# A first dense pair cut into chunks of 512, 512 and 128 tokens, with banks given out by first free

## The chip, the cores and the metric

The kernel runs on one core of a Trainium2 chip. The metric is the device time of one execution in microseconds. In the rows, PE is TensorE (matmuls; PEld its weight loads), DVE is VectorE, ACT is ScalarE, POOL is GpSimd and SP is the engine that issues most plain DMAs.

## What is computed

A small attention over 32 memory slots gives a row of 512 numbers for each of 4608 tokens. A mixture of 8 experts follows: each token goes to one expert, each expert takes 576 tokens, and runs two matrix products with a ReLU between them. Then one dense layer, the same for all tokens, with a product, a gate and a product:

```python
x = attn_out                      # 4608 x 512
for e in range(8):                # 576 tokens each, by sorted router logits
    h = np.maximum(x[mask_e] @ w1[e], 0.0)      # 512 -> 1024
    out[mask_e] = h @ w2[e]                     # 1024 -> 512
h = out @ w_in                    # 512 -> 2048
g = h * np.clip(h + 3.0, 0.0, 6.0) / 6.0
return g @ w_out                  # 2048 -> 512
```

Products run in two 16-bit parts of each operand, so each of them is three matmuls: high by high, high by low, low by high.

## The kernel before

The attention comes first (to about 230 us). Then experts are taken in pairs. For each expert `l1` makes 16 tiles of 288 tokens (12 matmuls each) and `l2` makes 8 (24 matmuls each); after both experts of a pair, `l34(P)` runs the dense layer over the pair's 1152 tokens. `l34` has three chunks of 384 tokens and, in each, 16 steps `f` of the hidden dimension. A step has an L3 part (12 matmuls with the 128x128 tiles of `w_in` as weights and the chunk's tokens moving, into one PSUM bank `p`) and an L4 part (3 matmuls for each 128 tokens, into accumulators `acc0` to `acc2` that live for the whole chunk). Between them the step is evicted: ScalarE makes the gate from `p`, VectorE multiplies it by `p` (which frees the bank), ScalarE casts the high part `g[:, 0]`, GpSimd subtracts to get the low part. `LAG = 2`: the L4 part of step n is issued after the L3 part of step n+2. At a chunk's end the accumulators go through ScalarE and VectorE and are scattered to the output.

Engines take their instructions in the order in which a planner wrote them down. The planner keeps a clock (`CK.now`) and an estimate of each engine's time (`V_`, `A_`, `G_`); generators for routing, gathering, weights and dense weights are run as side tasks while the matmuls are recorded, and a task goes on when the estimate says its turn has come. What is late on the chip against that plan makes the in-order queues wait.

Four side tasks matter here:

- `weights()` loads the 8 x 2 expert matrices into four staging buffers `wst0` to `wst3`, takes a scale (the matmul `amx` spreads the maximum over partitions) and converts them into `w_0` to `w_3`. W1[e] and W2[e] below are the first and second matrix of expert e.
- `route(k)` finds the tokens of the k-th expert: eight rounds of compare and count, then six one-hot tiles `OH` on VectorE, each used by six small matmuls `rtp`, and at the end the row numbers `ix`.
- `gathers()` fetches the token rows `xg` by an indirect DMA on GpSimd and transposes them (`xp`) into `xt`.
- `dense_piece` turns one of 32 pieces of `w_in` and `w_out` from their 64-bit words into two 16-bit parts. A piece has four VectorE instructions on a `cva` buffer (one TENSOR_SCALAR and three SCALAR_TENSOR_TENSOR), three on ScalarE and one subtract on GpSimd. Pieces of `w_out` can't be finished before their scale is known (`dmx`, after all of `w_out` has been looked through by `dm`). L3 of step f needs piece f of `w_in` (`WI[f]`), L4 needs piece f of `w_out`.

`ysplit` scales an expert's output for the dense layer: the maxima `ym` of its 8 tiles go into `sy_1m` for the second expert of a pair, and one matmul `amx` waits for that. This `amx` stands in TensorE's queue behind the first L3 matmuls of the chunk, though the first chunk holds only tokens of the pair's first expert.

PSUM has eight banks: four under the tag `mm` (all of `p`, `amx`, `xp`), `acc0` to `acc2`, and one for `rtp`. `mm` banks are given out in turn: a new tile waits for the oldest of the four.

Of the kernel before, what the change touches and what calls it, by code (L numbers as in the profile page):

```python
# [20 lines left out]
def attn_moe_kernel(ctx: ExitStack, tc: tile.TileContext, q, k, v, phi, w_gate, w1, w2, w_in, w_out, out):  # L21
    nc = tc.nc
# [67 lines left out]
    with tc.tile_pool(name="ald", bufs=2) as ald, tc.tile_pool(name="aw", bufs=2) as aw, \  # L90
# [322 lines left out]
        def x_mm(t, pool, tag, *gs):  # L413
            u, half = XO[t // 2], t % 2
            if gs != (1,):
                XP[t] = pool.tile([128, 2, 256], F32, name="xa", tag=tag, bufs={"qp": 2, "mm": 4}[tag])
# [212 lines left out]
    MMQ = []  # L629

    def mm_slot(done):
        while len(MMQ) >= 4:
            d = MMQ.pop(0)
            b, CK.busy = CK.busy, False
            need(lambda: d[0])
            CK.busy = b
        MMQ.append(done)

    def mm_tile(shape, name, done):
        mm_slot(done)  # L640
        return ps.tile(shape, F32, name=name, tag="mm", bufs=4)
# [23 lines left out]
    ones72 = rt.tile([128, 2 * NT], F32, name="ones72")  # L665
    nc.vector.memset(ones72, 1.0)
# [21 lines left out]
    def all_max(m, f, late=0.0):  # L688
        yield V_.t + HOP + late
        done = [False]  # L690
        while len(MMQ) >= 4 and not MMQ[0][0]:
            yield CK.now + 0.05
# [44 lines left out]
    def route(k):  # L737
# [136 lines left out]
        V_.tensor_tensor_scan(sc.rearrange("p a t -> p (a t)"), ones72, G.rearrange("p a t -> p (a t)"), 0.0,  # L874
# [51 lines left out]
        def oh(q4):  # L926
            o = rt.tile([128, 6, 128], BF16, name="OH", bufs=3)
# [3 lines left out]
        yield V_.t - 0.3  # L931
        OH = [oh(0)]
# [51 lines left out]
    def weights():  # L984
        for T in range(2 * E):
            k, which = divmod(T, 2)
            while k not in EIX or T == 3 and 1 not in XI:
                yield CK.now + 0.3
# [26 lines left out]
            for n in range(9):  # L1015
# [19 lines left out]
                elif n:  # L1035
# [5 lines left out]
                    if i and T + 1 < 2 * E and T != 2:  # L1041
                        w_issue(T + 1, c)
# [5 lines left out]
    XT, XI = {}, set()  # L1048
# [7 lines left out]
    def gathers():  # L1056
        for k in range(E):
# [7 lines left out]
            def fetch(i):  # L1065
# [3 lines left out]
                elif k == 1 and i > 1:  # L1069
                    if i % 2 == 0:  # L1070
                        big.append(wk.tile([128, 2, 512], F32, name="xg", tag=f"wst{i // 2 - 1}"))
                    xg = big[-1][:, i % 2]
                else:
                    xg = wk.tile([128, 512], F32, name="xg", tag=f"xg{i % 2}")
# [3 lines left out]
            depth = 2 if k > 1 else 5  # L1078
            big = []
# [7 lines left out]
            XI.add(k)  # L1087
# [4 lines left out]
            for i in range(5):  # L1092
# [4 lines left out]
                while len(MMQ) >= 4 and not MMQ[0][0]:  # L1097
# [49 lines left out]
    def spare(kind):  # L1147
        tags = ["dst0", "dst1", "dst2"] if kind else ["cva0", "cva1"]
        if 1 in XT or 1 in L1D:
            tags += [] if kind else ["xg0", "xg1"]  # L1150
# [102 lines left out]
    def x_tiles(n):  # L1253
        for _ in range(n):
# [4 lines left out]
            if g == 0:  # L1259
                XC[:] = [[False]]  # L1260
                mm_slot(XC[0])
            x_mm(t, ps, "mm", g)
# [130 lines left out]
    def l34(P):  # L1393
# [3 lines left out]
        acc = []  # L1397

        def l4(n):
# [3 lines left out]
            if f == 0:  # L1403
                acc[:] = [ps.tile([128, 512], F32, name=f"acc{t}") for t in range(3)]
            need(lambda: ok[0] >= 1)
            for i, (wi, xi) in enumerate(((0, 0), (1, 0), (0, 1))):
                if xi == 1:
                    need(lambda: ok[0] >= 2)
                for t in range(3):
                    mm(acc[t], g[:, xi, t * 128:t * 128 + 128], WO[f][:, wi], f == 0 and i == 0, f == 15 and i == 2,  # L1410
                       fp16(512))
            if f == 15:
                a3 = list(acc)
# [121 lines left out]
```

## Time and profile before

| | us |
|---|---|
| median of 3 runs | 1510.31 (1505.42 to 1511.45) |
| the profiled execution | 1503.65 |
| its span, first to last instruction | 1501.6 |
| TensorE busy in it | 1397.4 (93%) |
| VectorE busy | 835.3 (56%) |
| ScalarE busy | 732.6 (49%) |
| GpSimd busy | 487.8 (32%) |

The stages around the change, in the profiled execution: L1 of the first expert ends near 291 us, its L2 runs to 324, the second expert's L1 to 351 and its L2 to 380; the first dense chunk runs from there to about 456, the whole first dense pair to about 585. From 456 on TensorE is busy nearly without a gap until the end.

### The profile page before, as it was taken

To read this page: it belongs to the slowest core of one execution; us is meant where nothing else is said; L and a number is where in the kernel's file an instruction comes from. 1 tells how busy PE (TensorE), PEld (TensorE's weight loads), DVE (VectorE), ACT (ScalarE), POOL (GpSimd) and SP (SyncE) were. 2 spreads that over 40 slices of the span, in tenths; PEclk is the share of its full clock that TensorE was granted. 3 is DMA by queue.
4 is the path that set the end of the run, shared out by engine and by line. 5 is a ranking of instruction groups with operands and counts; after the bars stand their busy time and mean duration, and the time that the engine had idled before them with its cause. 6 is when DMAs were issued, how large, how long until landed. Compare 5 with 4: busy or idle time off the path is not lost.

```text
span 1501.6 us, 26275 instructions
## 1 busy us (share of the span) xinstructions
PE 1397.4 (93%) x10506; PEld 931.4 (62%) x10506; DVE 835.3 (56%) x1985; ACT 732.6 (49%) x1419; POOL 487.8 (32%) x555
## 2 busy tenths in 40 slices
PE   4778886898889999999999999999999999999997
PEld 3667764777444555997555558875555588755553
DVE  4788967889995775553146755522459335221111
ACT  3667655577763563452335634523346445233332
POOL 3565305134553443301233532102325421023232
PEclk9989996999999999999999999999999999999999
DMA  9866587355310221200001311100013211000000
GB/s 299 293 231 201 158 273 248 118 185 167 114 43 22 82 84 57 86 28 2 1 22 57 109 57 51 64 1 1 22 57 110 71 39 62 1 0 22 1 21 21
DMA packets 65913, 130.67 MB, mean 87 GB/s; under 512 B 5248, under 2 KB 35968, under 8 KB 65792
## 3 DMA queue, kind: packets, MB, share of 16 engines
q1 hardware_dynamic: 49808, 74.48, 15.0%
q0 software_dynamic: 15168, 52.96, 10.9%
q8 instruction: 82, 1.34, 0.4%
q10 hardware_dynamic: 816, 1.57, 0.3%
q14 instruction: 39, 0.32, 0.1%
HBM read 110.12 MB, written 18.87 MB: 86 GB/s over the span
## 4 chain that ended last, share of the span: by engine, by line
PE 67%; DVE 14%; ACT 5%; issue 5%; DMA 4%; POOL 2%; SPq 0%; ACTq 0%; POOLq 0%; DVEq 0%
PE p L618 39%; PE acc L618 21%; DVE cva L567 4%; DMA xg<-xd,ix 2%; PE xa L420 1%; DMA ph<-in_phi_dram 1%; PE kvp L191 1%; DMA wst<-in_moe_w_dram,ei 1%; DVE w L567 1%; ACT h L567 1%; PE rtp L795 1%; DVE pm L138 1%; PE xp L623 1%; DVE h L567 1%; POOL h L567 1%
## 5 line engine op out<-in xcount | busy, mean ns | idle before, releaser
L618 PE MATMUL acc<-wo,h 128*128 128x512 f16 x1728 | 418.1, 379 | 5.2 <-ACT h L567 4.3
L618 PE MATMUL p<-yt,wi 128*128 128x384 f16 x2304 | 417.6, 327 | 0.0
L567 POOL TENSOR_TENSOR h<-h,h 128x384 f16<-128x384 f32 x192 | 187.3, 976 | 634.5 <-ACT h L567 492.6
L618 PEld LDWEIGHTS <-w 128*128 128x128 f16 x3072 | 339.1, 121 | 49.1 <-issue 4.4
L618 PEld LDWEIGHTS <-wi 128*128 128x128 f16 x2304 | 219.2, 98 | 156.0 <-issue 1.2
L567 ACT ACTIVATE h<-p,half_c,inv 128x384 f32<-128x384 f32 (+1 forms) x256 | 143.9, 587 | 278.5 <-PE p L618 271.2
L618 PEld LDWEIGHTS <-h 128*128 128x128 f16 x1728 | 163.5, 98 | 174.1 <-ACT h L567 6.0
L567 DVE SCALAR_TENSOR_TENSOR h<-h,p 128x384 f32<-128x384 f32 x192 | 105.9, 551 | 290.0 <-ACT h L567 282.7
L618 PE MATMUL p<-xt,w 128*128 128x288 f16 x1536 | 198.8, 289 | 3.7 <-DVE h L567 3.5
L618 PE MATMUL p<-h,w 128*128 128x288 f16 x1536 | 196.3, 287 | 4.3 <-DVE w L567 3.7
L567 ACT ACTIVATE h<-h 128x384 f16<-128x384 f32 x192 | 100.1, 521 | 135.7 <-DVE h L567 131.9
L567 DVE SCALAR_TENSOR_TENSOR h<-p,h 128x288 f16<-128x288 f32 x128 | 57.4, 455 | 73.6 <-ACT h L567 73.5
L567 DVE SCALAR_TENSOR_TENSOR w<-wst,s,w 128x512 f16<-128x512 f32 x124 | 96.1, 806 | 2.2 <-ACT w L567 2.2
L567 POOL DMA_INDIRECT wst<-in_moe_w_dram,ei x64 | 68.7, 1073 | 87.0 <-DVE scn L567 33.5
L567 ACT ACTIVATE h<-p 128x288 f16<-128x288 f32 x128 | 51.7, 410 | 90.8 <-PE p L618 90.8
L567 ACT ACTIVATE w<-wst,s 128x512 f16<-128x512 f32 x124 | 82.5, 712 | 7.1 <-DVE s L567 6.2
L567 DVE SCALAR_TENSOR_TENSOR cva<-dst,cva 128x512 int32<-128x512 int32 (+1 forms) x96 | 82.7, 881 | 0.5 <-ACT dst L567 0.3
L567 DVE TENSOR_REDUCE ym<-y 128x1 f32<-128x288 f32 x64 | 28.8, 450 | 91.5 <-ACT y L567 91.3
L567 ACT ACTIVATE wscr<-wst 128x1024 bf16<-128x1024 f32 x64 | 67.3, 1052 | 13.3 <-DMA wst<-in_moe_w_dram,ei 12.6
L567 ACT ACTIVATE y<-p 128x288 f32<-128x288 f32 x64 | 26.1, 407 | 96.6 <-PE p L618 95.1
L567 POOL DMA_INDIRECT xg<-xd,ix x35 | 37.2, 1064 | 75.9 <-PE xp L623 49.7
L191 PE MATMUL kvp<-kvt,A 128*64 128x128 f32 x576 | 46.0, 315 | 7.3 <-ACT A L170 3.3
(313 smaller groups left out, 1558.4 us busy)
## 6 DMA issues: line engine op xcount, KB each, us to landing
dst<-in_moe_w_out_dram SPq DMA_DIRECT2D x26, 512.0 KB, 4.3
qt<-in_q_dram SPq DMA_DIRECT2D x8, 1024.0 KB, 11.5
dq<-in_moe_w_in_dram SPq DMA_DIRECT2D x16, 512.0 KB, 5.7
xd<-xs SPq DMA_DIRECT2D x32, 256.0 KB, 5.5
kvt<-in_k_dram SPq DMA_DIRECT2D x7, 1152.0 KB, 9.1
kvt<-in_v_dram SPq DMA_DIRECT2D x7, 1152.0 KB, 11.8
dst<-in_moe_w_in_dram SPq DMA_DIRECT2D x15, 512.0 KB, 4.0
ph<-in_phi_dram SPq DMA_DIRECT2D x8, 576.0 KB, 9.8
```

Of the source, the lines that this page charges most:

```text
L138: nc.vector.tensor_reduce(pm, PH[b].rearrange("p h (r m) -> p h m r", m=M), axis=AX.X, op=OP.max)
L191: nc.tensor.matmul(p[i * 64:(i + 1) * 64, g, 0:128], A[:, hp, r, :], KV[b][:, :, hp, r * 64:(r + 1) * 64], start=(r == 0), stop=(r == R - 1))
L420: nc.tensor.matmul(p[r, g], AT[u][:, half, g, r], VB[b][:, g], start=True, stop=True)
L567: r = f(*a, **kw)
L618: nc.tensor.matmul(o, l, r, start=start, stop=stop)
L623: nc.tensor.transpose(o, i, idn)
L795: nc.tensor.matmul(p[:60, :32], C[:, 4 * t:4 * t + 4].rearrange("p t n -> p (t n)"), Bo[:, 4 * t:4 * t + 4].rearrange("p t e -> p (t e)"), ...
```

## The change

- The first dense pair (`P == 0`) is cut into chunks of 4, 4 and 1 times 128 tokens; the other pairs keep 3, 3, 3. A chunk of 512 has four accumulators, and the fourth takes one of the four `mm` banks for as long as the chunk lasts. The accumulators are evicted last first, so the bank comes back early. In the last chunk the L4 part lags three steps instead of two.
- `mm` banks have tags of their own (`mm0` to `mm3`), and a new tile takes any that is free, the longest unused first.
- The one-hot tiles of the second routing round are held until W2[0] has been converted, and `OH` has two buffers instead of three.
- Row fetches have three buffers (`xg0` to `xg2`) and go three deep; the second expert's fetches no longer borrow `wst0` and `wst1`, so W2[1] no longer waits for them. `xg2` also serves as one more `cva` buffer. A constant of ones is reused.

```diff
+    MMS, MMU, MMN = [None] * 4, [0] * 4, [0]
+    def mm_free():
+        return [i for i in range(4) if MMS[i] is None or MMS[i][0]]
     def mm_slot(done):
-        while len(MMQ) >= 4:
-            d = MMQ.pop(0)
-            b, CK.busy = CK.busy, False
-            need(lambda: d[0])
-            CK.busy = b
-        MMQ.append(done)
+        b, CK.busy = CK.busy, False
+        need(mm_free)
+        CK.busy = b
+        i = min(mm_free(), key=lambda i: MMU[i])
+        MMN[0] += 1
+        MMS[i], MMU[i] = done, MMN[0]
+        return f"mm{i}"
...
-            o = rt.tile([128, 6, 128], BF16, name="OH", bufs=3)
+            o = rt.tile([128, 6, 128], BF16, name="OH", bufs=2)
...
         yield V_.t - 0.3
+        while k == 1 and 0 not in W2:
+            yield CK.now + 0.1
         OH = [oh(0)]
...
-            while k not in EIX or T == 3 and 1 not in XI:
+            while k not in EIX:
...
-                    if i and T + 1 < 2 * E and T != 2:
+                    if i and T + 1 < 2 * E:
                         w_issue(T + 1, c)
...
-            depth = 2 if k > 1 else 5
+            depth = 3 if k else 5
...
+        CN = (4, 4, 1) if P == 0 else (3, 3, 3)
+        CT = (0, CN[0], CN[0] + CN[1])
...
-                acc[:] = [ps.tile([128, 512], F32, name=f"acc{t}") for t in range(3)]
+                acc[:] = [ps.tile([128, 512], F32, name=f"acc{t}") for t in range(min(3, CN[ch]))]
+                held[:] = [[False]]
+                if CN[ch] > 3:
+                    acc.append(mm_tile([128, 512], "acc3", held[0]))
...
-                    for t in range(3):
-                        T = 3 * ch + t
+                    for t in reversed(range(len(a3))):
+                        T = CT[ch] + t
...
-            if n >= LAG:
-                l4(n - LAG)
+            lag = LAG if n < 32 or P else 3
+            while nx[0] <= n - lag:
+                l4(nx[0])
+                nx[0] += 1
```

The planner sets the order, so the diff moves more than it names. Three places follow. In the names, the number is a buffer's own.

VectorE at the end of the first expert's L1, before: the last two tiles of W2[0] (`w_2`, `w_3`) are converted ahead of the last steps of the second routing round (`mi` to `ce`).

```order
L567 SCALAR_TENSOR_TENSOR w_2_4027<-wst_3675,s_0_3903,w_2_4027 128x512
L567 SCALAR_TENSOR_TENSOR w_3_4075<-wst_3699,s_0_3903,w_3_4075 128x512
L567 TENSOR_SCALAR FL<-rtp 15x8
L567 SCALAR_TENSOR_TENSOR w_3_4075<-wst_3699,s_0_3903,w_3_4075 128x512
L567 SCALAR_TENSOR_TENSOR cva<-dst,cva 128x512
L567 TENSOR_REDUCE mi<-rtp 128x1
L567 TENSOR_SCALAR fp<-mi,fp 128x1
L567 TENSOR_SCALAR G<-V,fp 128x36
```

The same place now:

```order
L567 SCALAR_TENSOR_TENSOR sli<-sl,sl_4206 128x36
L567 TENSOR_SCALAR lo<-sli 128x36
L567 TENSOR_SCALAR hi<-sli 128x36
L567 TENSOR_TENSOR R_4213<-hi,iTf 128x180
L567 TENSOR_TENSOR RH<-R_4213,idt 128x360
L567 SCALAR_TENSOR_TENSOR w_2_4151<-wst_3673,s_0_3901,w_2_4151 128x512 x2
L567 SCALAR_TENSOR_TENSOR w_3_4219<-wst_3697,s_0_3901,w_3_4219 128x512 x2
L567 SCALAR_TENSOR_TENSOR cva<-dst,cva 128x512
L567 TENSOR_TENSOR OH<-lo,i_2717 128x768
```

W2[0] is now finished behind the whole of the routing round but its one-hot tiles, because its `amx` gets a free bank 46 matmuls later.

VectorE, the scale of `w_out` (`dmx`, `dmm`), before: it stands among the one-hot tiles, and its rows come after the routing round.

```order
L567 TENSOR_REDUCE dm_89<-dst 128x1
L567 TENSOR_REDUCE ym<-y_4282 128x1
L567 TENSOR_TENSOR OH<-lo,i_2717 128x768
L567 TENSOR_SCALAR s_1m<-ws_4367 128x1
L567 TENSOR_REDUCE dmx_4405<-dm_89 128x1
```

Now:

```order
L567 SCALAR_TENSOR_TENSOR cva<-dst,cva 128x512
L567 CAST CS<-rtp 60x32
L567 TENSOR_REDUCE dm_89<-dst 128x1
L567 TENSOR_SCALAR cva<-dst 128x512
L567 TENSOR_REDUCE dmx_4006<-dm_89 128x1
L567 TENSOR_SCALAR FL<-rtp 15x8
```

It now stands inside the routing round, in the place that W2[0] left, so pieces of `w_out` can be converted earlier: 88 of the 128 `cva` instructions stand ahead of `sy_1m` now, 76 before; 25 ahead of the last `ym` of the first expert now, 17 before; and 39 of them between `sy_1m` and the last conversion now, 51 before.

ScalarE at the turn from the second dense chunk to the third, before:

```order
L567 ACTIVATE w_3_6803<-wst_6605,s_2_6693 128x512
L567 ACTIVATE h_6806<-h_6809 128x384
L567 ACTIVATE h_6876<-p_6846,half_c,inv_5964 128x384
L567 ACTIVATE h_6873<-h_6876 128x384
L567 ACTIVATE h_6908<-p_6890,half_c,inv_5964 128x384
L567 ACTIVATE xt<-xp,sx 128x4x128
L567 ACTIVATE h_6905<-h_6908 128x384
L567 ACTIVATE xt<-xp,sx 128x4x128
L567 ACTIVATE y_6956<-acc_6111,inv_5338 128x512
L567 ACTIVATE y_6960<-acc_6113,inv_5964 128x512
```

Now (`h<-p` is the gate of a step, `h<-h` its cast, `y<-acc` an accumulator's eviction):

```order
L567 ACTIVATE h_7156<-p_7123,half_c,inv_6007 128x128
L567 ACTIVATE h_7122<-h_7127 128x128
L567 ACTIVATE w_1_7165<-wst_6787,s_2_7076 128x512 x2
L567 ACTIVATE w_2_7179<-wst_6801,s_2_7076 128x512
L567 ACTIVATE h_7151<-h_7156 128x128
L567 ACTIVATE w_2_7179<-wst_6801,s_2_7076 128x512
L567 ACTIVATE h_7217<-p_7200,half_c,inv_6007 128x128
L567 ACTIVATE w_3_7222<-wst_6876,s_2_7076 128x512 x2
L567 ACTIVATE h_7214<-h_7217 128x128
L567 ACTIVATE y_7253<-acc_6178,inv_6007 128x512
L567 ACTIVATE y_7269<-acc_6177,inv_6007 128x512
L567 ACTIVATE y_7273<-acc_6175,iv_5371 128x512
```

The eight casts of W2[2] (two of `w_0` stand just ahead of these rows) now lie inside the first steps of the short third chunk, and the eviction of `acc0`, the only accumulator that chunk uses, stands behind them.

## Rows read from the trace of the kernel before

**Rows 1.** Busy time by stretch: us, then PE, PEld, DVE, ACT, POOL; clock, DMA

```profile
269.90:345.00 75.10, 67.16 (x575) 57.43 (x574) 67.63 (x166) 47.77 (x96) 22.50 (x20) 1.00 0.44 141
345.00:390.00 45.00, 34.92 (x259) 26.60 (x257) 44.83 (x75) 32.12 (x60) 21.21 (x15) 0.96 0.55 176
390.00:445.20 55.20, 50.89 (x263) 25.78 (x263) 54.44 (x76) 40.22 (x71) 31.41 (x25) 0.97 0.23 67
455.70:515.00 59.30, 59.02 (x409) 30.09 (x408) 31.44 (x96) 23.86 (x49) 19.68 (x21) 1.00 0.14 50
```

**Rows 2.** TensorE in order of time: start, us, what, [idle before <-releaser]

```profile
292.88 0.28 PE L618 MATMUL p<-h,w 128*128 128x288 f16 x1 [0.61 <-ACT h L567]
...
324.37 2.12 PE L618 MATMUL p<-xt,w 128*128 128x288 f16 x16
...
354.51 0.91 PE L618 MATMUL p<-h,w 128*128 128x288 f16 x6 [1.41 <-DVE w L567]
357.71 22.55 PE L618 MATMUL p<-h,w 128*128 128x288 f16 x169 [2.28 <-DVE w L567]
380.09 4.55 PE L618 MATMUL p<-yt,wi 128*128 128x384 f16 x27
390.09 0.77 PE L694 MATMUL amx<-ident,sy_1m 128*128 128x128 f32 x2 [5.45 <-DVE sy_1m L567]
```

**Rows 3.** What TensorE waited for, 390.6 to 456 us: total, times, longest

```profile
PE acc L618 <- ACT h L567: 4.3, 4, 1.8
PE acc L618 <- POOL h L567: 0.3, 1, 0.3
```

**Rows 4.** VectorE in order of time, same columns as rows 2

```profile
288.42 0.73 DVE L567 SCALAR_TENSOR_TENSOR w<-wst,s,w 128x512 f16<-128x512 f32 x1
...
389.79 0.15 DVE L567 TENSOR_SCALAR sy_1m<-sy_1m 128x1 int32<-128x1 int32 x1
```

**Rows 5.** VectorE by shape, 325 to 446 us: count, busy us, mean ns

```profile
L567 DVE SCALAR_TENSOR_TENSOR cva<-dst,cva 128x512 int32<-128x512 int32 x56 | 52.1, 941 | 0.1
L567 DVE SCALAR_TENSOR_TENSOR cva<-dst,cva 128x512 f32<-128x512 f32 x28 | 23.7, 845 | 0.0
L567 DVE TENSOR_SCALAR cva<-dst 128x512 int32<-128x512 int32 x27 | 17.9, 662 | 0.0
L567 DVE SCALAR_TENSOR_TENSOR h<-h,p 128x384 f32<-128x384 f32 x13 | 7.1, 543 | 0.0
```

**Rows 6.** VectorE by shape, 269.8 to 297 us, and (last row) 297 to 325

```profile
L567 DVE SCALAR_TENSOR_TENSOR cva<-dst,cva 128x512 int32<-128x512 int32 x4 | 2.7, 686 | 0.0
L567 DVE SCALAR_TENSOR_TENSOR cva<-dst,cva 128x512 f32<-128x512 f32 x2 | 1.4, 703 | 0.0
...
L567 DVE TENSOR_SCALAR cva<-dst 128x512 int32<-128x512 int32 x1 | 0.4, 416 | 0.0
```

**Rows 7.** What VectorE waited for, 269.9 to 345 us

```profile
DVE xt L567 <- ACT xt L567: 2.3, 2, 1.2
DVE CS L567 <- PE rtp L795: 1.7, 2, 1.1
```

**Rows 8.** TensorE in steady dense work, and in the attention

```profile
705.79 2.11 PE L618 MATMUL acc<-wo,h 128*128 128x512 f16 x9
707.74 2.11 PE L618 MATMUL p<-yt,wi 128*128 128x384 f16 x12
709.69 2.11 PE L618 MATMUL acc<-wo,h 128*128 128x512 f16 x9
...
141.87 0.23 PE L341 MATMUL sc<-km,qh 128*128 128x64 f16 x2
...
142.20 0.19 PE L341 MATMUL sc<-km,ql 128*128 128x64 f16 x1
```

**Rows 9.** ScalarE by shape: 480 to 600 us, and (last row) 325 to 446

```profile
L567 ACT ACTIVATE w<-wst,s 128x512 f16<-128x512 f32 x16 | 10.5, 710 | 0.5 <-DVE s L567 0.5
L567 ACT ACTIVATE h<-p,half_c,inv 128x192 f32<-128x192 f32 x20 | 9.1, 503 | 14.5 <-PE p L618 14.5
L567 ACT ACTIVATE y<-acc,inv 128x512 f32<-128x512 f32 x2 | 1.4, 688 | 0.0
...
L567 ACT ACTIVATE yt<-y,sy 128x64 f16<-128x64 f32 x4 | 1.3, 332 | 0.0
```

**Rows 10.** What TensorE waited for, 480 us to the end

```profile
PE xp L623 <- DMA xg<-xd,ix: 2.1, 4, 1.0
```

## What the change should do to the time

> **What bounds the kernel now.** I read the busy time by stretch first [rows 1], to see which engine is full where. From 345 to 445 us VectorE is busy 99 of 100 us and TensorE is not; before that, from 270 to 345, VectorE still has 75.1 - 67.6 = 7.5 us to spare; after 456 TensorE is busy 59.0 of 59.3. So the program has a stretch of some 100 us that VectorE paces, with the dense pieces, and then 1000 us that TensorE paces. In the second part only matmuls count. In the first, only what delays the moment from which TensorE never waits again.
>
> Then TensorE in order of time [rows 2] shows where it loses in the first part: 1.41 + 2.28 us in the second expert's L2 for W2[1], and 5.45 us for sy_1m, the scale that stands in its queue behind 27 matmuls of the first dense chunk. What TensorE waited for [rows 3] adds 4.3 + 0.3 = 4.6 us inside that chunk. All of these end on VectorE or on what follows it. By shape [rows 5], the cost there is the conversions: 56, 28 and 27 instructions, 94 of the 121 us.
>
> **The change, part by part.**
>
> Columns. The pair has the same 1152 tokens. A step of a 384 chunk starts 9 L4 matmuls every 1.95 us and 12 L3 matmuls every 1.95 us [rows 8], so 217 ns for 512 columns and 162 for 384. Before: 48 steps of 3.90 = 187.2 us. After: 32 steps of 24 x 0.217 = 5.20 (166.4) and 16 short ones. A short step has 3 L4 matmuls (0.65) and 12 L3 matmuls of 128 columns, which the trace does not show. The nearest rows are 64 columns, where the 1st and the 12th start 0.33 us apart, so 30 ns each with a weight load of its own [rows 8], and 384 columns at 162; on the line between them 128 columns take 56. So 12 x 0.056 + 0.65 = 1.33 us, 21.2 for 16, and 187.6 in all: +0.4 us. The bounds are 30 ns (-5.0 us over 192 matmuls, which the columns themselves exclude) and 60 ns, a whole 64-column spacing for each half (+0.8).
>
> One rule speaks against the short chunk. The Trainium skill, "TensorE: Matmul & The Clock Gate", section "Back-to-back issue gap", gives about 81 ns as the sustained spacing at 128 columns, since the weight load sets it too; the same sentence gives 131 ns at 512 columns, where this trace has 217. As an estimate from that page the short chunk would cost 192 x 25 ns = 4.8 us more.
>
> The wait for sy_1m. Banks by first free lets the matmul loop of the first L1 take every bank as it comes free, and `amx` for W2[0] comes 46 matmuls later. Its eight conversions leave the routing round, and the scale of w_out takes their place. Hence 12 more conversion instructions, three pieces, stand in VectorE's queue ahead of sy_1m (88, not 76). They are not extra work, only earlier work, but what stands behind them waits: W2[1] (11 more ahead of its end), `ym`, sy_1m, and then TensorE. Price of three pieces: at best 3 x (0.416 + 2 x 0.686 + 0.703) = 7.5 us [rows 6], at worst, as between 325 and 446, 3 x (0.662 + 2 x 0.941 + 0.845) = 10.2 [rows 5]. Eight of the twelve stand ahead of the last `ym` of the first expert, where the low prices hold, so two thirds at 7.5 and one third at 10.2: 8.4 us. They could fall into VectorE's 7.5 us of idle time, which would make them nearly free. I do not count on it: that idle time ends on ScalarE's half of the token tiles and on round trips of the routing [rows 7], and the new order keeps both. W2[0] itself now ends behind the routing round. I put it near 299 us, where it ended at 289 [rows 4]; the first L2 would start at its time (293, [rows 2]), stand still for some 5 us, and be paced by the six one-hot tiles. This lies under VectorE's queue and is not added again. So sy_1m moves from 389.8 [rows 4] to about 398: **+8.4 us**, bounds 0 and 10.2.
>
> What is already done by then. 23 L3 matmuls of 512 stand ahead of that `amx` (5.0 us), where 27 of 384 stood (4.4). With the +0.4 above: **-0.2 us**.
>
> The waits inside the first chunk. VectorE's queue between sy_1m and the last conversion had 55.2 us [rows 1] for 13 steps, 4.25 each, against TensorE's 3.90; with two steps of lag that had to end in waits. Now it has 12 conversions less (12 x 0.83 = 10) and 8 evictions of 512, some 0.7 us each, for 13 of 0.543: 54.4 - 10 - 7.1 + 5.5 = 43 us, 5.35 for a step of 5.20. It falls behind by 1.2 us in all, and the lag of two steps covers 10. The 4.6 us go: **-4.6**.
>
> The turn to the short chunk. Its only accumulator is `acc0`, which is evicted last. From the end of the second short L3 to its first L4, TensorE has 2 x 2.6 + 2 x 0.68 = 6.6 us of work. In that time ScalarE has, in its order, eight weight casts, two gates, three casts of 128 columns and three evictions. Rows: a cast 0.71, an eviction 0.69, 0.33 for 64 columns and 0.50 for 192 [rows 9], so about 0.42 for 128. Casts in a row start 0.66 apart: 5.3 + 5 x 0.42 + 3 x 0.69 = 9.5, begun about 0.5 early when the scale comes: 9.0 against 6.6. **+2.4 us**, bounds 0 (the scale comes early) and 5. The fourth accumulator leaves three `mm` banks in the long chunks; a bank is held for some 2 us of a 5.20 us step, so that costs nothing. At the first turn there are no weight casts, and three evictions (2.1) fit under one L3 (2.6).
>
> The other pairs. Three row buffers can save at most the 2.1 us that TensorE waits for rows after 480 us [rows 10]; I take half: **-1.0**.
>
> Sum: 8.4 - 0.2 - 4.6 + 2.4 - 1.0 = **+5.0 us**. Against the profiled execution's own 1503.65 that is 1508.7; the median of the runs shown lies 6.7 us above it, and the forecast is made on the median: 1510.3 + 5.0 = **1515.3**. About 0.5%, 7.5 us, is what a measurement of this kernel can tell from no change.
>
> **Rivals.**
>
> A. ScalarE becomes the bound of the short chunk (slower). Its 16 steps have 21.2 us on TensorE. ScalarE has 16 x 2 x 0.42 = 13.4, casts 5.3 to 5.7 and four evictions 2.8: 21.5 to 21.9. If a 128-column instruction takes over (21.2 - 8.3) / 32 = 0.40 us, ScalarE is full, each step's chain of four engines no longer fits under three steps of lag (4.0 us), and late evictions come back as TensorE waits. Price 5 us on top of the forecast: 1520.3. For it: the 0.33 at 64 columns, which leaves little. Against: the casts lie in the first third, and after that each step needs 0.84 of 1.33.
>
> B. VectorE hides the earlier pieces (faster). If the 12 conversions do fall into the 7.5 us of idle time, the pieces left behind W2[1] shrink by the same time, and the waits for W2[1] and sy_1m (3.7 + 5.5) shrink instead of growing: up to -9.1 in place of +8.4, so 1510.3 - 9.1 - 0.2 - 4.6 + 2.4 - 1.0 = 1497.8, and half of that way 1506.6. For it: DMA and ScalarE have room before 325 us. Against: at 345 us VectorE is full and its queue is longer by what the order shows.
>
> C. The weight load sets the pace at 128 columns (slower). If a 128-column matmul can't start while its weights come in, the load comes on top of its 56 ns, at most the 30 ns of a whole 64-column matmul: 192 x 30 ns = 5.8 us, 1521.1. For it: no row at 128. Against: 64 columns at 30 ns leave no place for a load that isn't hidden. This is the direction of the Trainium skill's page named above.
>
> D. The change doesn't do what it says: the first chunk goes on waiting for pieces, since VectorE's evictions, late by the 8.4 us, drag it. The 4.6 stay: 1519.9.
>
> **How the numbers follow.** Forecast (from 1508 to 1518, by the bounds of the wait and the turn): 0.54. A 0.18, B 0.18, C 0.05, D 0.05. A, C and D are slower than 1517.8 (+0.5%), as is a little of the forecast's own range (0.02): slower 0.30. B in its full size is faster than 1502.8, in its half size not: 0.14 faster, and 0.04 of it within. Within 0.5%: 0.54 - 0.02 + 0.04 = 0.56. The range: upward to A and C with half of their spread, 1523; downward half of the way into B's better part, 1502. Left out is about 0.1 below and 0.08 above.
>
> **What would show it.** In the new profile: the first L2 starts near 293 us and waits on VectorE until about 299; the wait for W2[1] ends near 366; `amx` for sy_1m starts at 398, not 390; no wait on `acc` follows in the first chunk; VectorE's last conversion ends where it did, 441 to 446; short L3 matmuls start 56 ns apart; one wait of 2 to 3 us on `y` stands at the second turn. I am wrong on the main term if `amx` starts before 394, and on the sign if it starts before 390. I am wrong on the turn if that wait is over 5 us or if waits on `acc` go on through the short chunk.

## The result, and the profile after

The changed kernel's median is 1519.96 us (1517.38 to 1526.13, 6 runs), that of the kernel before 1505.99 (1501.62 to 1511.45, 6 runs) beside it: a ratio of 1.0091, 95% interval 1.0063 to 1.0119. It is slower by some 14 us. The profiled execution took 1518.47, span 1516.5, which is 14.9 more than before.

The forecast was made on three runs of the kernel before, with a median of 1510.3, some 4 us above what more runs gave. So the forecast 1515.3 looks closer than its working was: that said +5.0, and the change made +14.0. The same holds for the range: 1502 to 1523 is -8.3 to +12.7 us around 1510.3, and +14.0 lies outside it.

Busy time by stretch in the changed kernel (us; then PE, PEld, DVE, ACT, POOL; clock, DMA) answers to [rows 1]:

```profile
270.00:345.00 75.00, 59.47 (x479) 48.54 (x478) 59.52 (x151) 40.05 (x79) 24.81 (x18) 0.91 0.41 135
345.00:445.00 100.00, 87.48 (x517) 54.84 (x516) 98.80 (x155) 74.43 (x135) 49.80 (x34) 0.91 0.37 116
```

From 345 to 445 VectorE is as full as before. From 270 to 345 it is not: 59.5 us busy where it had 67.6, and TensorE 59.5 where it had 67.2, with the clock at 0.91 where it was 1.00. The queue has more conversions for this stretch, and yet VectorE does less in it. TensorE in order of time (start, us, what, count, [idle before <-releaser]) shows where, beside [rows 2]:

```profile
291.14 1.88 PE L618 MATMUL p<-h,w 128*128 128x288 f16 x14 [0.18 <-DVE h L567]
295.36 0.30 PE L618 MATMUL p<-h,w 128*128 128x288 f16 x1 [2.34 <-DVE w L567]
298.82 0.32 PE L955 MATMUL rtp<-RH,OH 128*128 128x10 bf16 x6 [3.16 <-DVE OH L567]
...
314.94 0.32 PE L955 MATMUL rtp<-RH,OH 128*128 128x10 bf16 x6 [5.64 <-DVE OH L567]
315.13 5.69 PE L618 MATMUL p<-h,w 128*128 128x288 f16 x25
...
335.71 3.96 PE L618 MATMUL p<-xt,w 128*128 128x288 f16 x31
...
364.29 1.39 PE L618 MATMUL p<-h,w 128*128 128x288 f16 x6 [3.11 <-DVE w L567]
367.75 1.62 PE L618 MATMUL p<-h,w 128*128 128x288 f16 x6 [2.07 <-DVE w L567]
371.87 22.30 PE L618 MATMUL p<-h,w 128*128 128x288 f16 x169 [2.50 <-DVE w L567]
394.01 5.13 PE L618 MATMUL p<-yt,wi 128*128 128x512 f16 x23
403.96 0.77 PE L695 MATMUL amx<-ident,sy_1m 128*128 128x128 f32 x2 [4.83 <-DVE sy_1m L567]
```

The first L2 begins at 291.1 and waits 2.3 and 3.2 us, about as forecast. Then comes a wait of 5.64 us at 314.94 that I had not foreseen, and behind it 25 matmuls in 5.69 us, 228 ns each, where the 169 of the second expert's L2 take 132: the granted clock is 0.50 there for a while, 1.2 GHz, the lower of its two levels (1.2 and 2.4). The second expert's L1 starts 11.3 us later than in [rows 2], `amx` for sy_1m 13.9 later.

Who waits at 314.94 is read back engine by engine, VectorE first, then ScalarE, then GpSimd (POOL):

```profile
304.24 0.95 DVE L567 TENSOR_TENSOR OH<-lo,i 128x768 bf16<-128x768 int32 x1
313.23 0.45 DVE L567 TENSOR_REDUCE ym<-y 128x1 f32<-128x288 f32 x1 [8.04 <-ACT y L567]
313.60 0.42 DVE L567 TENSOR_SCALAR cva<-dst 128x512 int32<-128x512 int32 x1
313.94 0.95 DVE L567 TENSOR_TENSOR OH<-lo,i 128x768 bf16<-128x768 int32 x1
```

```profile
311.75 1.06 ACT L567 ACTIVATE wscr<-wst 128x1024 bf16<-128x1024 f32 x1 [9.42 <-DMA wst<-in_moe_w_dram,ei]
312.72 0.19 ACT L567 ACTIVATION_READ_ACCUMULATOR wscr<-wst 128x1 f32 x1
312.81 0.39 ACT L567 ACTIVATE y<-p 128x288 f32<-128x288 f32 x1
```

```profile
296.73 5.54 POOL L567 DMA_INDIRECT wst<-in_moe_w_dram,ei  x1 [18.07 <-DVE w L567]
302.57 1.08 POOL L567 DMA_INDIRECT wst<-in_moe_w_dram,ei  x1 [0.30 <-DVE ym L567]
303.96 1.17 POOL L567 DMA_INDIRECT wst<-in_moe_w_dram,ei  x1 [0.30 <-issue]
305.44 0.94 POOL L567 DMA_INDIRECT wst<-in_moe_w_dram,ei  x1 [0.30 <-issue]
```

The sixth one-hot tile stands on VectorE behind a `ym`, `ym` waits 8.0 us for an eviction `y` on ScalarE, and `y` stands there behind the squares `wscr` of W1[1], which wait 9.4 us for W1[1] to land. Its four fetches are on GpSimd, the first at 296.73 behind a conversion `w`. In the kernel before the first was at 294.19 and the squares at 298.77, 13 us earlier (GpSimd, then ScalarE):

```profile
294.19 0.95 POOL L567 DMA_INDIRECT wst<-in_moe_w_dram,ei  x1 [7.69 <-DVE ei L567]
298.77 1.06 ACT L567 ACTIVATE wscr<-wst 128x1024 bf16<-128x1024 f32 x1 [1.71 <-DMA wst<-in_moe_w_dram,ei]
```

The order of the fetches says why (GpSimd's instructions in the changed kernel, with buffer numbers):

```
140 L567 DMA wst2_4222<-in_moe_w1_dram,ei1_4170 128x1024
141 L567 DMA wst3_4227<-in_moe_w1_dram,ei1_4170 128x1024
142 L567 DMA wst0_4230<-in_moe_w1_dram,ei1_4170 128x1024
143 L567 DMA wst1_4243<-in_moe_w1_dram,ei1_4170 128x1024
```

W1[1] goes into the staging buffers that W2[0] leaves. W2[0] is converted late; when its tiles 2 and 3 are, the expert number `ei` is already known, so these two are fetched first. Buffers 0 and 1 had been free since 289, but their fetches stand behind, and the squares begin with tile 0, which is fetched third.

Not all of the 15.2 us up to sy_1m (151.5 against 136.3 from the first L1 matmul) is waiting. TensorE in that stretch, before and then changed:

```profile
253.78:390.09 136.31, 116.59 (x941) 95.40 (x940) 125.89 (x277) 88.58 (x172) 46.11 (x37) 0.96 0.50 162
252.50:403.96 151.46, 121.80 (x937) 97.31 (x936) 131.99 (x289) 93.55 (x180) 55.98 (x40) 0.89 0.48 155
```

It is idle for 10.0 us more and busy for 5.2 us more, with nearly the same number of matmuls; the longer columns of the first chunk are some 0.6 of that. The rest, some 4.6 us as an estimate, goes with the granted clock, 0.89 against 0.96.

### The profile page after: what moved, and what is told of

Read it like the earlier page. It is cut to its first block, busy times and chain, and to the rows that moved or that the text cites. A ratio compares the mean times of both kernels' runs of the same rounds, so it can differ in the third digit from the quotient of the medians.

```text
span 1516.5 us, 26270 instructions
## 1 busy us (share of the span) xinstructions
PE 1403.0 (93%) x10506; PEld 926.3 (61%) x10506; DVE 833.8 (55%) x1983; ACT 732.0 (48%) x1420; POOL 485.1 (32%) x556
## 3 DMA queue, kind: packets, MB, share of 16 engines
q1 hardware_dynamic: 49808, 74.48, 14.9%
## 4 chain that ended last, share of the span: by engine, by line
PE 71%; DVE 14%; ACT 5%; issue 4%; DMA 3%; POOL 2%; SPq 0%; ACTq 0%; POOLq 0%; DVEq 0%
PE p L618 41%; PE acc L618 21%; DVE cva L567 4%; PE xa L420 2%; DVE w L567 2%; DVE h L567 1%; PE rtp L796 1%; ACT h L567 1%; DMA kvt<-in_v_dram 1%; PE xp L623 1%; PE kvp L191 1%; DMA wst<-in_moe_w_dram,ei 1%; POOL h L567 1%; DVE pm L138 1%; DVE ql L330 1%
## 5 line engine op out<-in xcount | busy, mean ns | idle before, releaser
L618 PE MATMUL p<-yt,wi 128*128 128x384 f16 (+2 forms) x2304 | 420.0, 328 | 0.0
L567 POOL TENSOR_TENSOR h<-h,h 128x384 f16<-128x384 f32 (+2 forms) x192 | 182.3, 951 | 649.1 <-ACT h L567 506.6
L618 PEld LDWEIGHTS <-wi 128*128 128x128 f16 x2304 | 213.6, 98 | 163.3 <-issue 4.1
L567 ACT ACTIVATE h<-p,half_c,inv 128x192 f32<-128x192 f32 (+5 forms) x256 | 144.1, 588 | 289.1 <-PE p L618 276.0
L567 DVE SCALAR_TENSOR_TENSOR h<-h,p 128x384 f32<-128x384 f32 (+2 forms) x192 | 105.8, 551 | 310.2 <-ACT h L567 302.3
L618 PE MATMUL p<-h,w 128*128 128x288 f16 x1536 | 202.0, 292 | 10.2 <-DVE w L567 10.0
L567 ACT ACTIVATE h<-h 128x384 f16<-128x384 f32 (+2 forms) x192 | 100.0, 521 | 126.7 <-DVE h L567 118.4
## 6 DMA issues: line engine op xcount, KB each, us to landing
qt<-in_q_dram SPq DMA_DIRECT2D x8, 1024.0 KB, 12.7
```

Source lines behind the costliest of these rows:

```text
L567: r = f(*a, **kw)
L618: nc.tensor.matmul(o, l, r, start=start, stop=stop)
```

## The experiments

Each run starts its expert part at another time, since the attention ahead varies (the first L1 matmul is at 252.5 to 259.2 us). So places are given from the first L1 matmul of the run (the first `p<-xt,w`) to the first matmul of `amx` for sy_1m, and from there to the span's end. "Ahead" is the number of `cva` instructions ahead of sy_1m on VectorE. Each profile is one execution; the changed kernel and e4, which differ only in the chunks, put sy_1m at 151.5 and 152.0. The sums, of one execution each, and the ratios, of 4 to 12, differ by up to 4 us: e3 is 20.2 us above the kernel before by its sum and 16.1 by its ratio. A step of 1 to 3 us in the sums alone is therefore only a hint. Expectations that give times of the changed kernel's profile are compared after taking off its 252.5 us.

| kernel | ahead | to sy_1m | sy_1m to end | sum | ratio to before (95%) |
|---|---|---|---|---|---|
| before | 76 | 136.3 | 1111.5 | 1247.8 | 1 |
| changed | 88 | 151.5 | 1112.5 | 1264.0 | 1.0091 (1.0063 to 1.0119) |
| e1 amx first | 74 | 137.2 | 1114.9 | 1252.0 | 1.0021 (0.9993 to 1.0048) |
| e2 fetch order | 86 | 143.0 | 1115.1 | 1258.1 | 1.0062 (1.0041 to 1.0084) |
| e3 in turn | 84 | 150.9 | 1117.1 | 1268.0 | 1.0107 (1.0075 to 1.0139) |
| e4 chunks of 384 | 88 | 152.0 | 1107.5 | 1259.5 | 1.0070 (1.0048 to 1.0091) |
| f1 e1 and e4 | 74 | 138.6 | 1110.2 | 1248.8 | 1.0003 (0.9984 to 1.0021) |
| f2 e1, `xp` later | 74 | 136.1 | 1113.1 | 1249.2 | 0.9990 (0.9972 to 1.0009) |
| f3 e2, w_out late | 76 | 136.7 | 1117.5 | 1254.1 | 1.0039 (1.0019 to 1.0059) |
| f4 no hold | 85 | 145.2 | 1117.0 | 1262.2 | 1.0105 (1.0076 to 1.0134) |
| g1 f2, 16 pieces | 64 | 130.9 | 1117.4 | 1248.3 | 0.9984 (0.9961 to 1.0007) |
| g2 f2, 14 pieces | 56 | 128.7 | 1118.7 | 1247.4 | 0.9981 (0.9956 to 1.0005) |
| g3 g1 with 384 | 64 | 131.6 | 1120.1 | 1251.7 | 1.0020 (0.9998 to 1.0042) |
| g4 g2, rows five deep | 56 | 132.8 | 1115.2 | 1248.1 | 1.0016 (0.9996 to 1.0036) |

**e1: a waiting `amx` gets the next bank.**

```diff
-        need(mm_free)
+        need(lambda: len(mm_free()) > MMW[0])
...
+        MMW[0] += 1
         while not mm_free():
             yield CK.now + 0.05
+        MMW[0] -= 1
         p = mm_tile([128, 128], "amx", done)
```

> The changed kernel, but a waiting amx is given the next bank that comes free, ahead of the matmul loop. Theory (the late amx of W2[0] starts it all; its conversions then hold the staging buffers in which W1[1] is fetched, and ScalarE, VectorE and TensorE wait in turn for that fetch): amx of W2[0] goes back from 281.8 us to about 273, W2[0] is converted by about 288, the four fetches of W1[1] start at about 293 and its first squares at about 298 instead of 311.8, no wait of TensorE over 2 us between 290 and 320, amx of sy_1m at about 389 instead of 404. With the waits of the first chunk gone (4.0 us) and about 4 us of new stalls at the turns, the span is 1498 to 1503, ratio to the kernel before 0.997 to 1.001. Rival 1 (the cut into 512, 512, 128 itself costs the time, from 404 us on): ratio stays at 1.006 or more even with sy_1m at 390.

The `amx` of W2[0] comes 21.1 us after the first L1 matmul (before 20.7, changed 29.3), the first squares of W1[1] at 44.5 (before 45.0, changed 59.3), sy_1m at 137.2. The front is that of the kernel before. The ratio fell to 1.0021, a little above what I expected; the 3.4 us from sy_1m to the end remain. So the late `amx` starts the loss of the front, and a smaller one lies behind it.

**e2: the fetches of W1[1] in the order 0, 1, 2, 3.**

```diff
-                        w_issue(T + 1, c)
+                        for cc in range(c + 1):
+                            w_issue(T + 1, cc)
```

> The changed kernel, but the fetches of W1[1] stand in the order 0, 1, 2, 3 in GpSimd's queue and not 2, 3, 0, 1, so that the two whose staging buffers come free first aren't behind the other two. amx of W2[0] stays late (281.8) and 86 conversion instructions still stand ahead of sy_1m (88 in the changed kernel, 76 before). Theory (the fetch is what my prediction missed, and the longer VectorE queue is what it priced): first squares of W1[1] at 296 to 300, no 8.0 us wait of VectorE on y, the wait of 5.6 us for the last one-hot tile gone; sy_1m at 397 to 399, so 5 to 6 us off the time: ratio 1.005. Rival 2 (VectorE's longer queue is the whole 14 us, its idle time at 305 to 313 only shows it early): sy_1m stays at 402 to 404, ratio 1.008 to 1.010. Rival 3 (the fetch is the whole loss, the longer queue costs nothing): sy_1m at 390 to 393, ratio 0.999 to 1.001.

W2[0] is as late as in the changed kernel. What VectorE waited for from 285 to 335 (total, times, longest):

```profile
DVE cva L567 <- POOL wi L567: 3.5, 2, 2.4
DVE ym L567 <- ACT y L567: 1.1, 2, 0.8
```

The longest wait for `y` is 0.8 us in place of 8.0, the last one-hot tile is not waited for, the squares start at 48.5 (47.5 at the latest was expected), and sy_1m comes 8.5 us earlier than in the changed kernel, at 143.0, where the theory had 144.5 to 146.5. The ratio is 1.0062 against the theory's 1.005; the other two lie outside its interval or at its edge. What remains, 143.0 - 136.3 = 6.7 us at sy_1m, is left for the longer queue. With the order, two conversions went from ahead of sy_1m (86 for 88).

**e3: banks in turn again.**

```diff
+    MMA = [None]
...
     def mm_free():
-        return [i for i in range(4) if MMS[i] is None or MMS[i][0]]
+        i = min((i for i in range(4) if i != MMA[0]), key=lambda i: MMU[i])
+        return [i] if MMS[i] is None or MMS[i][0] else []
...
+                    MMA[0] = max(range(4), key=lambda i: MMU[i])
...
+                            MMA[0] = None
```

> The changed kernel, but banks are given out in turn again (a new tile waits for the one used longest ago, the held fourth accumulator apart). My prediction named first free as what makes the amx of W2[0] late. Theory (not the choice of the bank, but that a waiting amx no longer gets in while the matmul loop waits): the amx still stands 46 matmuls later, at 281 to 282 us, sy_1m at 400 to 404, ratio 1.007 to 1.010. Rival 4 (first free is the cause): amx at about 274, sy_1m at 390 to 393, ratio 0.998 to 1.002.

`MMA` is the bank that the fourth accumulator holds. The `amx` of W2[0] stays where the changed kernel has it (29.3), sy_1m at 150.9, ratio 1.0107. Which bank is taken isn't the cause. In the kernel before, the matmul loop took the oldest entry off the list and then waited for it; meanwhile the list had a place, and a waiting `amx` got in. The new code looks for a free bank in both places, and the loop always looks first. e1, which gives the `amx` its turn and leaves the choice of banks as it is, agrees: what was lost is the turn.

**e4: chunks of 384 for the first pair.**

```diff
-        CN = (4, 4, 1) if P == 0 else (3, 3, 3)
+        CN = (3, 3, 3)
...
-            lag = LAG if n < 32 or P else 3
+            lag = LAG
```

> The changed kernel with the first dense pair in three chunks of 384 as before (lag of two steps throughout). Theory: the front is the same, sy_1m at 404; the first chunk has waits on acc again, of 3 to 5 us, the turn (1.0) and the stall of 3.2 us at 569 are gone: ratio 1.008 to 1.011, about the same as the changed kernel's 1.009. Rival 1 (the cut is what costs the time): ratio 1.003 or less.

The ratio 1.0070 lies between the two expectations (its interval reaches into the theory's), 0.0021 below the changed kernel's, though their intervals overlap. From sy_1m to the end it takes 1107.5, 5.0 us less than with the new cut. Waits on `acc` for ScalarE's `h` are back, 2.7 us, but of the waits after 520 us the stall at `xp` (`<-issue`), those for `CS` and the one at the turn (`y`) are gone. What TensorE waited for in the changed kernel, 520 to the end:

```profile
PE xp L623 <- issue: 3.2, 1, 3.2
PE rtp L805 <- DVE CS L567: 1.7, 2, 0.9
PE xp L623 <- DMA xg<-xd,ix: 1.2, 3, 0.8
PE acc L618 <- ACT y L567: 1.0, 1, 1.0
```

And e4, the same stretch:

```profile
PE xp L623 <- DMA xg<-xd,ix: 1.0, 3, 0.4
PE rtp L796 <- DVE C L567: 0.9, 2, 0.5
```

So by these two runs the cut itself costs 3 to 5 us (0.0021 of the ratio is 3.2, the sums differ by 4.5), of which 3.2 stand at one transposition `xp`. The intervals alone don't show it; f1 does it again.

**f1: e1 and e4 together.** Both edits above, nothing else.

> e1 (a waiting amx gets the next bank) and three chunks of 384 (e4) together: both parts that the two runs showed as losses are gone. Theory (the two losses add up: from the first L1 matmul to the end e1 took 1252.0 us and e4 gained 4.5 us against the changed kernel by its chunks): 1252.0 - 4.5 = 1247.5 us from the first L1 matmul, where the kernel before took 1247.8; no stall of 3 us at a transposition xp of the third expert; ratio 0.997 to 1.001. Rival (the chunks of 384 gain only behind the late front, where the dense pieces are further ahead): 1251 to 1253 us, ratio 1.001 to 1.003.

The sum is 1248.8 us, ratio 1.0003: nearer to the theory's 1247.5 than to the rival's 1251. With both losses undone the kernel takes what it took before, within what can be measured (some 3 us to either side). What else the change does (first free, the hold, three row buffers, W2[1] without waiting for rows) is still in f1 and leaves no loss that can be seen.

**f2: e1, with `xp` of the third expert after the second chunk.**

```diff
+            while k == 2 and YP.get(0, 0) < 2:
+                yield CK.now + 0.3
             xt = wk.tile([128, 2, 4, CAP], F16, name="xt")
```

> e1 with chunks of 512, 512, 128, but the transpositions xp of the third expert are held until the second chunk's L3 is through, so that they don't ask for banks while acc3 holds one of four. Theory (the 3.2 us stall of TensorE before the third xp is a wait for a bank, and what follows it a half clock): the stall goes, from sy_1m to the end 1114.9 us become 1110 to 1112. Rival (xp waited for its row, gathered late on GpSimd): a stall of the same size stays at some xp, 1114 to 1116 us from sy_1m to the end.

The stall goes, but sy_1m to the end is 1113.1, between theory and rival: in this execution only 1.8 us are won of 3 to 5, in part since the eviction of `acc0` at the turn is waited for 1.9 us where it was 1.0. The timed runs say more: the ratio goes from e1's 1.0021 to 0.9990, some 4.7 us, though the intervals overlap a little. Here is the stall in the changed kernel, TensorE and then VectorE:

```profile
565.03 1.04 PE L618 MATMUL p<-yt,wi 128*128 128x512 f16 x4
569.29 1.03 PE L623 MATMUL xp<-ident,xg 128*128 128x128 f32 x4 [3.22 <-issue]
570.12 3.00 PE L618 MATMUL p<-yt,wi 128*128 128x512 f16 x7
```

```profile
565.14 0.17 DVE L567 TENSOR_REDUCE mi<-rtp 128x1 int32<-128x8 f32 x1 [1.41 <-PE rtp L814]
565.91 1.86 DVE L567 TENSOR_SCALAR TH<-KT,fp 128x15 int32<-128x15 int32 x1
568.45 1.41 DVE L567 SCALAR_TENSOR_TENSOR xt<-xp,sx,xt 128x512 f16<-128x512 f32 x2
```

The third `xp` starts 0.1 to 0.2 us after the first of the two evictions `xt` could have freed a bank (568.45 + 0.7), and `acc3` holds the fourth. The seven matmuls behind it take 0.43 us each, twice their time. That a bank was missing fits this, f1 and f2, but f2 moves the rows' use too, and the trace names no releaser (`<-issue`). Whether the row was late instead isn't settled.

**f3: e2, with the scale of `w_out` held.**

```diff
+        while which and L2D.get(0, 0) < 2:
+            yield CK.now + 0.3
         a = absmax(DMX[which], f"dmx{which}")
```

> e2 (fetch order 0, 1, 2, 3, amx of W2[0] still 46 matmuls late), with the scale of w_out held until the second half of the first expert's L2, so that 76 conversion instructions stand ahead of sy_1m as in the kernel before, not 86 as in e2. Theory (each conversion instruction ahead of sy_1m costs its time in VectorE's queue, which is my prediction's main term): e2's 143.0 us from the first L1 matmul to the amx of sy_1m become 136 to 138 (10 instructions of 0.6 to 0.8 us). Rival (the queue has idle time, and the late W2[0] costs those 6.7 us by TensorE's waits for it and for the one-hot tiles): 141 to 144.

With 76 instructions ahead, as before, sy_1m comes at 136.7, 6.4 us earlier than in e2, though W2[0] is still late. So the longer queue is a price of its own, 0.64 us for each of ten, if the conversions alone made the difference; the scale of `w_out`, its `amx` and the order around them moved with them. But 2.4 of the 6.4 come back behind sy_1m, 2.0 of them as waits on `acc` in the first chunk (4.8 us against 2.8 in e2).

**f4: the changed kernel without the hold.**

```diff
-        while k == 1 and 0 not in W2:
-            yield CK.now + 0.1
```

> The changed kernel without the hold: the one-hot tiles of the second routing round aren't held until W2[0] is converted, and stand ahead of the last four of its conversions. Theory (the hold costs little; the order of the fetches does it): W2[0] ends some 5 us later, and so does the fetch of W1[1], whose tiles 2 and 3 still come first; first squares of W1[1] at 59 to 65 us from the first L1 matmul (59.3 in the changed kernel), sy_1m at 150 to 156, ratio 1.008 to 1.013. Rival (the hold is what delays the second expert): sy_1m at 140 to 146, ratio 1.002 to 1.005.

This went against my numbers for sy_1m: it comes at 145.2, 6.3 us earlier, which is the rival's place (140 to 146), and the squares of W1[1] at 57.5, not later. Yet the sum falls by 1.8 us only and the ratio is 1.0105, within the theory's range and outside the rival's. The hold shifts waits and isn't what the time hangs on. The run also says something of the stop of 8.0 us: it isn't there (VectorE's longest wait ahead of a `ym` from 290 to 340 is 1.2 us), though tile 0 of W1[1] is still fetched third. ScalarE has its first two `y` ahead of the squares here, where the changed kernel has one. Of the 4.5 us lost behind sy_1m, 2.9 are waits on `acc` in the first chunk (3.5 against 0.6); the rest I can't assign.

**g1 and g2: fewer pieces ahead of sy_1m.** f2, with the next dense piece started only when sy_1m is known, after 16 (g1) or 14 (g2) pieces.

```diff
-        for which, j in PO:
+        for i, (which, j) in enumerate(PO):
+            while i >= 16 and 1 not in SY:
+                yield CK.now + 0.1
```

> f2 (a waiting amx gets the next bank, xp of the third expert after the second chunk, chunks of 512, 512, 128), and after 16 of the 32 dense pieces the next one starts only when sy_1m is known: 64 conversion instructions ahead of sy_1m, where f2 has 74. Theory (each costs its 0.7 us in VectorE's queue, and TensorE's 5.3 us wait for sy_1m is made of them; the first chunk of 512 has room on VectorE for what comes later): 10 x 0.7 = 7 us, more than the wait, so the wait goes: from the first L1 matmul to the amx of sy_1m 129 to 131 us in place of 136.1, no more than 2 us of new waits on acc in the first chunk, ratio 0.995 to 0.997. Rival (the later pieces are wanted by the first chunk, which waits for them instead): waits on acc or wo of 4 us or more come up before 470 us, ratio 0.998 to 1.001.

> As g1, but only 14 pieces (56 conversion instructions) ahead of sy_1m. Theory: the wait for sy_1m is already gone with 16, so nothing more is won; two more pieces come later, which the 512 chunk still covers or just doesn't: the same ratio as g1, 0.995 to 0.998. Rival: L4 of the first chunk waits for pieces of w_out (5 are done at its start), 3 us or more, ratio 0.998 or higher.

sy_1m comes at 130.9 and 128.7, where f2 has 136.1. What TensorE waited for from 375 to 470 us, f2:

```profile
PE amx L697 <- DVE sy_1m L567: 5.3, 1, 5.3
PE acc L618 <- ACT h L567: 2.4, 3, 1.2
PE acc L618 <- POOL h L567: 0.9, 2, 0.6
```

and g2:

```profile
PE acc L618 <- ACT h L567: 8.2, 6, 2.1
PE acc L618 <- POOL h L567: 0.5, 1, 0.5
```

The wait changes its place: 8.6 us in all in f2, 8.7 in g2. In g1 the waits on `acc` are 7.0 us, and 2.1 are left at sy_1m. This is the rivals' result (0.9984 and 0.9981). Both kernels are faster than the changed one, and their medians lie below the kernel before, but the intervals reach 1.0007 and 1.0005, so neither is shown to be.

**g3: g1 with chunks of 384.**

```diff
-        CN = (4, 4, 1) if P == 0 else (3, 3, 3)
+        CN = (3, 3, 3)
```

> As g1, but with three chunks of 384 in the first dense pair. Theory (what the chunk of 512 buys is room on VectorE for pieces that come late: 5.2 us a step with 0.6 us of eviction, where 384 has 3.9 and 0.46): the first chunk waits for pieces, 4 to 8 us on acc, so the ratio is 0.998 to 1.001. Rival (late pieces fit there as well, and the turns of the 512 cut cost): 0.994 to 0.997, no worse than g1.

1.0020: L4 waits 2.9 us in one place for a piece of `w_out`, and the sum is 3.4 us above g1's. That fits a chunk of 512 that is worth its turns when pieces come late; with 74 ahead it wasn't (f1 against e1; f2 draws level). g3's interval and g1's overlap, so it is not shown.

**g4: g2 with rows five deep for the second expert.** The fourth and fifth row tile go into `wst0`, and W2[1] is fetched behind them.

```diff
-            while k not in EIX:
+            while k not in EIX or T == 3 and 1 not in XI:
...
+                elif k == 1 and i > 2:
+                    if i == 3:
+                        big.append(wk.tile([128, 2, 512], F32, name="xg", tag="wst0"))
+                    xg = big[-1][:, i - 3]
...
-            depth = 3 if k else 5
+            depth = 3 if k > 1 else 5
```

> g2, but the second expert's token rows are fetched five deep again as in the kernel before (three in xg0 to xg2, two in the staging buffer wst0, and W2[1] is fetched behind them). In g2 the fourth and fifth row wait for a buffer, and the last transposition xp waits 3.7 us, so the second expert's L1 starts 74.9 us after the first L1 matmul, where the kernel before has 70.6. Theory (three buffers are a loss for the second expert, whose rows are wanted at once): L1 of the second expert starts at 70.5 to 72, and as fewer pieces stand in VectorE's queue W2[1] comes in time (waits under 2 us): sy_1m at 124 to 127 in place of 128.7, ratio 0.995 to 0.997. Rival (the first chunk waits for the pieces instead, which come no earlier): the waits on acc before 470 us rise from 8.2 us to 11 or more, ratio 0.998 to 1.000.

The second expert's L1 starts at 70.6, as expected, but the waits for W2[1] are 4.7 us, not under 2, and sy_1m comes at 132.8. Ratio 1.0016: neither mechanism as I had it. What the deeper fetch wins in L1 is lost on W2[1], which comes behind it. So no cost of this part of the change, that W2[1] no longer waits for rows, can be seen here.

## Why the prediction was right or wrong

The sign that the sum gave was right and the range held the time; the size was not, and that the range held is luck: as a change from 1510.3 it reached to +12.7 us, and the change made +14.0. The time is within a microsecond of what rivals D (1519.9) and A (1520.3) gave, and neither's mechanism occurred. To a change within 0.5% I had given 0.56 and to a slower one 0.30; it is 0.9% slower. My signs of being wrong looked to one side only: `amx` before 394 or 390. It came at 404, the wait for W2[1] ended at 371.9 (forecast 366), and VectorE's last conversion at 449.9 (441 to 446).

**The columns** were right. Short steps follow each other by 1.32 us (forecast 1.33):

```profile
602.63 0.83 PE L618 MATMUL p<-yt,wi 128*128 128x128 f16 x12
603.30 0.81 PE L618 MATMUL acc<-wo,h 128*128 128x512 f16 x3
603.95 0.83 PE L618 MATMUL p<-yt,wi 128*128 128x128 f16 x12
```

12 matmuls of 128 columns start within 0.67 us, 56 ns each. That is not the 81 ns of the Trainium skill's page "TensorE: Matmul & The Clock Gate" ("Back-to-back issue gap"), nor is the rate at 512 columns, 216 ns, its 131. What the same section of the Trainium skill gives for a matmul by itself, about 56 and 216 ns, fits both. Rivals A and C fall with these rows.

**The wait for sy_1m** is the term that was mis-sized: +8.4 forecast, 13.9 us in the two traces, 15.2 counted from the first L1 matmul. Its own mechanism fits f3 against e2 and was nearly right in size: 6.4 us for ten instructions, where 8.4 stood for twelve. The step that failed is the sentence on W2[0]: the first L2 "would be paced by the six one-hot tiles. This lies under VectorE's queue and is not added again". I had followed W2[0]'s late end to TensorE, not to the staging buffers that it frees. The fetch of W1[1] hung on those, ScalarE's queue on the fetch, and VectorE's on ScalarE: VectorE's queue stood still itself, 8.0 us, so nothing lay under it. Undoing the order alone gives 8.5 us at sy_1m, of which the two conversions fewer are some 1.3 by f3's price, and 5.9 in the sum (e2). The stop hangs on more than the order, though: f4 keeps the order and has none, and as an estimate up to 4.6 of the 8.0 us came from the first fetch, which took 5.54 us where one in the kernel before took 0.95. How the 8.0 us divide stays open. The prediction also had no term for the clock, which by the estimate above is some 4.6 us of the 15.2. The fetch order stood in GpSimd's list with buffer numbers and could have been read beforehand.

**The cause I named** for the late `amx`, banks by first free, is not it (e3); the `amx` lost its turn (e1).

**The waits in the first chunk**: 4.6 us forecast to go, 4.0 went; 0.6 is left, against [rows 3]:

```profile
PE acc L618 <- POOL h L567: 0.6, 1, 0.6
```

But I gave this to the chunk as much as to the pieces. e1 has the same 512 chunk and 4.6 us of waits again. So the two terms, +8.4 and -4.6, look like largely one quantity: a piece moved ahead of sy_1m is one piece less behind it, and in g1 and g2 the wait moves the other way.

**The turn** cost 1.0 us, not 2.4, within its bounds. **The fourth accumulator**, which I costed at nothing ("a bank is held for some 2 us of a 5.20 us step"), is the other step that failed, as far as the runs show: with the cut some 3 us are lost (e4, f1: 3.2 and 2.7 by the ratios, 4.5 and 3.2 by the sums), most of it in one stall of 3.2 that I didn't foresee, and with `xp` moved away from the held bank the ratio is back at 0.9990 (f2). That the held bank is the cause is argued, not shown. I had only counted `p` tiles, not the transpositions of the next pair. **The other pairs** gave 0.9 of the 1.0: waits for rows after 480 us are 1.2 against 2.1 in [rows 10].

Rival B (the earlier pieces fall into idle time) and D (the waits in the first chunk stay) fall. My bounds for the wait, 0 to 10.2, had no room for a chain over three engines; the range held since it reached to A and C, which did not happen.

The sums make a ladder: changed 1264.0; fetch order 1258.1 (5.9); as many pieces ahead as before 1254.1 (4.0); W2[0] early 1252.0 (2.1); chunks of 384 1248.8 (3.2); the kernel before 1247.8, 1.0 left. The timed ratios fall along it too: 1.0091, 1.0062, 1.0039, 1.0021, 1.0003 (steps of 4.4, 3.5, 2.7 and 2.7 us); neighbours' intervals overlap, the ends' do not. The edits don't add up along it: e1 has neither e2's edit nor f3's, since an early W2[0] makes both needless.

## What to carry to other kernels

When a step moves later, list what it releases (buffers, banks, its place in a queue) and follow each to the next in-order queue, since a late fetch can stop there everything that stands behind its first reader. Pieces of work that are moved ahead of a critical point and come back as slack behind it are one term, not two. A free-bank search that several tasks share needs a rule for who is served first, or the busiest loop can take every bank.

## What the runs showed of the hardware

The first of the four fetches was recorded with 5.54 us where the others take about 1. It is the same in e3 and e4, and in e2 and f3 the third fetch takes 5.52. In all five it ends 0.8 us after VectorE's first gap, in the changed kernel the 0.36 us before this row:

```profile
301.80 0.45 DVE L567 TENSOR_REDUCE ym<-y 128x1 f32<-128x288 f32 x1 [0.36 <-ACT y L567]
```

(302.27 against 300.49 + 0.95 = 301.44.) The Trainium skill, "SBUF — State Buffer", section "SBUF: two separate sides", says that a fetch issued by GpSimd can't write its descriptors while VectorE runs certain operations that take the ports the two share. The trace agrees in part only: the next fetch, at 302.57, ran 1.08 us beside a VectorE that was just as full. And in f4 the second fetch is long and ends at 310.41, 0.25 us before VectorE's first gap of over 0.1 us (310.66):

```profile
307.17 3.24 POOL L567 DMA_INDIRECT wst<-in_moe_w_dram,ei  x1 [1.61 <-DVE w L567]
```

What the long fetch costs was not tried by itself.

Here a stall cost more than its length. After 5.6 us without a matmul, 25 matmuls took 228 ns each instead of 132: some 2.4 us more. The mean granted clock was 0.72 from 313 to 325 us, and 0.50 (1.2 GHz) from 315 to 318, where the kernel before had 1.00 (2.4 GHz). The same stretch, changed and then before:

```profile
313.00:325.00 12.00, 9.16 (x59) 6.56 (x60) 8.41 (x24) 8.61 (x16) 5.62 (x5) 0.72 0.32 109
313.00:325.00 12.00, 9.45 (x77) 7.55 (x76) 9.71 (x18) 7.39 (x13) 7.01 (x7) 1.00 0.48 128
```
